# Two fused layers on one core: the passage to the output products, the fill operands and the first pair reordered

## The chip, the core and the metric

One core of a Trainium2 chip runs the whole program in one launch. The metric is the device time in microseconds from start to end of an execution; several executions are timed and their median counts. TensorE is called PE here, VectorE DVE, ScalarE ACT, GpSimd POOL; SP is the engine whose queue issues nearly all DMAs.

## The reference

```python
def phi(x):                                   # q, k, v: 8 x 8 heads x 576 x 64; w_phi: 64 x 128
    proj = einsum('bhsd,df->bhsf', x, w_phi)
    proj = proj - max(abs(proj), axis=-1)
    return concatenate([exp(proj), exp(-proj)], axis=-1)
q_p, k_p = phi(q), phi(k)
kv, z = einsum('bhsf,bhsd->bhfd', k_p, v), k_p.sum(axis=2)
x = (q_p @ kv) / (q_p @ z + 1e-6)             # then 4608 tokens x 512
xn = x / sqrt(mean(x*x) + 1e-6) * rms_g
g, val = xn @ w_gate, xn @ w_val              # 512 -> 1536
out = (g * sigmoid(g) * val) @ w_out          # 1536 -> 512
```

## The kernel before, in words

All products run on PE in a split form of fp32: an operand x becomes a high part (a cast on ACT, line 60) and a low part (x minus the high part, line 61, on DVE or POOL), and a product is three matmuls: high by high, high by low, low by high.

**Attention (lines 190 to 550).** 32 pairs of heads pass through a software pipeline. `front` transposes k, q and the 64 rows left over of both (`rb`) on PE (line 298), splits them and projects them with w_phi (lines 311 to 313, one PSUM tile `pp` of two for each call of `proj`); DVE takes the maximum (315) and subtracts it (318). `mid` takes the exponentials on ACT (338, 378, 379), sums kv on PE (351), and POOL makes the low parts `ql` of q's features (383, 385). `back` multiplies with kv (418), sends the denominators through DRAM (`dd`, `dr`, `di`) and back as `rc`; `last` multiplies by `rc` (455, 456; for the last pair but one on POOL) and stores `xs`. A scheduler orders each engine's instructions in this stage by its own estimate of readiness.

**Fill products.** Into this stage are mixed the products of `xs` with the first three column blocks of w_gate and w_val, for 18 blocks of 256 tokens. `fill` (line 470) splits a block's operands (tile `xo`, two buffers) and returns six units of 12 matmuls each (line 487). `landed` calls it when at most 3 units are left (lines 532 and 533), and once more behind the loop (545). The six units left at the end of the attention stage, and eight more blocks, follow as ordered work.

**Gate and value products (lines 1085 to 1170).** From here a planner (`Flow`) writes every engine's order by hand-given durations; its instructions carry line 563 in the profile. For 9 blocks of 512 tokens and 9 column blocks each, `Unit` makes seven products of a fast 2 by 2 scheme (six matmuls each) in PSUM banks A, B, E; its result `h` (three buffers) is stored into the DRAM tensor `hs`. `scales` makes the token scales with two matmuls on PE ("T" tasks). In the last two blocks the freed weight buffers take the split operands of w_out (`make_o`, the last one built in the tile `x`), and `hload(0)` reads the first 256 tokens of `hs` back as one DMA of 1536 KB into the buffer of weight block 5; `hload(1)` follows in program order.

**Output products (lines 1164 to 1280).** The scheduler orders again. For each of 18 groups `gi` of 256 tokens, `operands` makes seven split operands out of the four blocks a11, a12, a21, a22 of h: casts on ACT, sums on DVE (1191 to 1199, tiles `st`), low parts of a11 and a12 on DVE, the other five on POOL. `omm` runs 18 matmuls for each of the seven products (126 a group) into `fp`, `gy`, `gz`, `gd`. The tiles of this stage lie at the addresses of tiles of the stage before: first 16 buffers `xo` of 3 KB, then the two `st`; those over the last-used `x` wait for it.

## Time and profile before

| | us |
|---|---|
| median of 3 runs | 1263.27 (1262.48 to 1271.12) |
| the profiled execution | 1265.73 |
| its span, first to last instruction | 1264.0 |
| PE busy in the span | 1221.1 (97%) |
| attention with the mixed fill products | about 0 to 494 |
| fill products behind it | about 494 to 560 |
| gate and value products | about 560 to 988 |
| output products | 991.3 to 1259 |

A row of the timeline gives the start, the duration, the engine, the line, the operation with output and inputs, a count where several are merged, and in brackets how long the engine sat idle before it and what released it. Matmuls overlap, so a merged row's duration is longer than the sum of the starts' distances.

### The profile page before, as it was taken

How to read it: one execution, taken by the hardware profiler on the slowest of the kernel's cores; microseconds unless marked ns; L12 is line 12 of the kernel's file. 1: busy time of each engine (PE TensorE's matmuls, PEld its weight loads, DVE VectorE, ACT ScalarE, POOL GpSimd, SP SyncE). 2: the span in 40 equal slices, each digit the busy share in tenths (PEclk: the TensorE clock that was granted, in tenths of full speed). 3: DMA queues.
4: the chain of work that ended last, by engine and by line, in shares of the span. 5: the costliest groups of instructions: out<-in, count | busy, mean ns of one | idle time of the engine just before them, and what ended most of it. 6: DMA issues, size and time to landing. Idle time of an engine off the chain costs nothing.

```text
span 1264.0 us, 28426 instructions
## 1 busy us (share of the span) xinstructions
PE 1221.1 (97%) x10355; PEld 1206.9 (95%) x10355; DVE 1040.8 (82%) x1495; ACT 803.5 (64%) x1865; POOL 836.9 (66%) x758
## 2 busy tenths in 40 slices
PE   7999999999999998999999999999999699999998
PEld 6998999999999998899999999999999699999998
DVE  6888987788878885387986988798876789999994
ACT  5887887778787894666566666667656343434341
POOL 3655665555665666764876875676566578888884
PEclk9999999999999999999999999999999899999999
DMA  5455576565666637675365556655545445444521
GB/s 150 132 127 152 144 200 174 159 176 153 183 167 171 175 102 220 184 239 175 127 200 195 182 194 203 200 176 181 183 146 167 144 147 165 139 134 160 166 93 51
DMA packets 214297, 206.55 MB, mean 163 GB/s; under 512 B 70287, under 2 KB 176655, under 8 KB 214157
## 3 DMA queue, kind: packets, MB, share of 16 engines
q1 hardware_dynamic: 214156, 204.73, 53.7%
q8 instruction: 82, 1.34, 0.4%
q14 instruction: 59, 0.48, 0.1%
HBM read 135.18 MB, written 69.49 MB: 162 GB/s over the span
## 4 chain that ended last, share of the span: by engine, by line
PE 54%; DVE 3%; DMA 1%; issue 1%; POOL 1%; ACT 1%; DVEq 0%; ACTq 0%; POOLq 0%
PE B L563 12%; PE E L563 10%; PE A L563 10%; PE gd L1241 6%; PE gz L1241 6%; PE gy L1241 5%; PE fp L1241 3%; PE fp L487 1%; DMA hs<-h 1%; PE fp L563 1%; DVE wc L563 1%; DMA gvs<-fo 1%; POOL xo L61 0%; PE S L563 0%; DVE xo L61 0%
## 5 line engine op out<-in xcount | busy, mean ns | idle before, releaser
L383 POOL TENSOR_TENSOR ql<-eq,qh 128x256 fp32r<-128x256 f32 x256 | 219.3, 887 | 84.5 <-ACT qh L379 43.4
L563 PE MATMUL B<-xo,w 128*128 128x256 f32 x1458 | 195.0, 278 | 3.9 <-ACT h L563 1.9
L563 PEld LDWEIGHTS B<-xo,w 128*128 128x128 f32 x1458 | 179.4, 188 | 5.3 <-DVE c L563 2.8
L61 POOL TENSOR_TENSOR xo<-st,xo 128x768 fp32r<-128x768 f32 x54 | 126.4, 2355 | 39.9 <-ACT xo L60 38.1
L563 POOL TENSOR_TENSOR h<-h,c 128x256 f32<-128x256 f32 x81 | 65.4, 808 | 114.2 <-ACT h L563 87.2
L60 ACT CAST xo<-st 128x768 fp32r<-128x768 f32 x54 | 43.5, 836 | 150.6 <-DVE st L1194 73.4
L563 PE MATMUL A<-xo,w 128*128 128x256 f32 x972 | 137.7, 277 | 0.3 <-ACT B L563 0.3
L563 PE MATMUL E<-xo,w 128*128 128x256 f32 x972 | 137.7, 277 | 0.0
L315 DVE TENSOR_REDUCE mx<-pp 128x4 f32<-128x512 f32 (+1 forms) x160 | 100.8, 632 | 42.7 <-PE pp L313 41.0
L351 PE MATMUL acc<-vm,ek 128*128 128x65 f32 x1024 | 130.0, 269 | 0.3 <-ACT ek L338 0.2
L351 PEld LDWEIGHTS acc<-vm,ek 128*128 128x128 f32 x1024 | 126.0, 193 | 0.9 <-ACT ek L338 0.9
L563 PEld LDWEIGHTS A<-xo,w 128*128 128x128 f32 x972 | 123.3, 188 | 0.8 <-ACT B L563 0.5
L563 PEld LDWEIGHTS E<-xo,w 128*128 128x128 f32 x972 | 123.1, 188 | 0.2 <-DVE h L563 0.2
L379 ACT ACTIVATE qh<-sm 128x512 fp32r<-128x512 f32 (+1 forms) x192 | 97.3, 507 | 0.0
L61 POOL TENSOR_TENSOR xo<-w,xo 128x768 fp32r<-128x768 f32 x36 | 91.6, 2544 | 0.0
L311 PE MATMUL pp<-wh,th 128*128 128x256 f32 x288 | 87.2, 304 | 4.6 <-DVE yr L318 2.6
L378 ACT ACTIVATE eq<-sm 128x512 f32<-128x512 f32 x128 | 78.5, 614 | 16.5 <-PE sm L367 16.5
L313 PE MATMUL pp<-wh,tl 128*128 128x256 f32 x288 | 83.5, 297 | 0.0
L312 PE MATMUL pp<-wl,th 128*128 128x256 f32 x288 | 81.3, 283 | 0.0
L385 POOL TENSOR_TENSOR ql<-eqr,qh 128x256 fp32r<-128x256 f32 x32 | 24.6, 767 | 81.9 <-ACT qh L379 77.5
L1241 PE MATMUL gy<-w,xo 128*128 128x256 f32 x648 | 77.8, 278 | 0.2 <-ACT xo L60 0.2
L338 ACT ACTIVATE ek<-yk 128x512 f32<-128x512 f32 x128 | 75.4, 650 | 3.9 <-DVE yk L318 3.8
(188 smaller groups left out, 3560.9 us busy)
## 6 DMA issues: line engine op xcount, KB each, us to landing
w<-hs SPq DMA_DIRECT2D x18, 1536.0 KB
hs<-h SPq DMA_DIRECT2D x81, 256.0 KB
gvs<-fo SPq DMA_DIRECT2D x108, 128.0 KB
gvr<-gvs SPq DMA_DIRECT2D x54, 256.0 KB
x<-xs SPq DMA_DIRECT2D x18, 512.0 KB
x<-xs SPq DMA_DIRECT2D x9, 1024.0 KB
rc<-di SPq DMA_DIRECT2D x31, 288.0 KB
kt<-in_k_dram SPq DMA_DIRECT2D x32, 256.0 KB
```

The costliest lines, as they stand in the source:

```text
L61: (lo_eng or nc.vector).tensor_tensor(lo, x, hi.bitcast(F32), ALU.subtract)
L311: nc.tensor.matmul(o, th[:, cs], wh, start=True, stop=False)
L312: nc.tensor.matmul(o, th[:, cs], wl, start=False, stop=False)
L313: nc.tensor.matmul(o, tl[:, cs], wh, start=False, stop=True)
L315: nc.vector.tensor_reduce(mx[:, 0:2 * m], pp[:, 0:2 * m], axis=AX.X, op=ALU.max, apply_absolute_value=True)
L338: nc.scalar.activation(e[h][:, sg], y["k", h], AF.Exp, scale=1.0 - 2.0 * sg)
L351: nc.tensor.matmul(acc[:, sg, h], e[h][:, sg, j], vm[:, h, j], start=False, stop=(h == 1 and j == T0 - 1))
L378: nc.scalar.activation(ei[:, sg], yi, AF.Exp, scale=1.0 - 2.0 * sg)
L379: nc.scalar.activation(hi[:, sg], yi, AF.Exp, scale=1.0 - 2.0 * sg)
L383: nc.gpsimd.tensor_tensor(lo[:, sg, cs], ei[:, sg, cs], hi[:, sg, cs].bitcast(F32), ALU.subtract)
L563: r = f(*a, **k)
L1241: nc.tensor.matmul(place[n], a[:, kp], w[:, o], start=(first and kp == 0 and i == 0), stop=(kp == KP - 1 and i == 2), skip_group_check=True)
```

## The change

It does eight things. (1) The first pair's `front` is in the order k, q, k's projections, then the left-over rows and q. (2) `landed` is called when at most 6 units are left; behind the loop only when fewer than 6 are. (3) A "T" task counts as ready 0.8 us later for the planner. (4) `hload(0)` is four DMAs of 384 KB with points of the unit order as their earliest places; `hload(1)` is a task of the planner. (5) Four of nine `xo` buffers of the gate stage and eight of sixteen of the output stage are skipped at first, and `st` lies ahead of `xo`, so that the buffers used first lie elsewhere. (6) In the first group the low parts of s2 and s3 go to DVE, and its first sum is recorded behind the last instructions of the other engines, so that the low parts of a11 and a12 stand ahead of it. (7) In the first group `omm` takes the high-by-high and high-by-low matmuls of the first five pieces first. (8) The last group's last sum is in two halves.

```diff
-        return [lambda: trans("r" if pr else "k"), lambda: trans("k" if pr else "r"),
+        if pr == 0:
+            return [lambda: trans("k"), lambda: trans("q"), lambda: proj("k", 0), lambda: proj("k", 2),
+                    lambda: trans("r"), lambda: proj("r", 0), lambda: proj("q", 0), lambda: proj("q", 2)]
+        return [lambda: trans("r"), lambda: trans("k"),
...
-        if len(units) <= 3:
+        if len(units) <= 6:
             landed(nc.vector if i < PR else nc.gpsimd)
...
-    if here:
+    if here and len(units) < 2 * J1:
...
-            r = max([0.0] + [d["done"] + self.HOP for d in deps])
+            r = max([0.0] + [d["done"] + self.HOP for d in deps]) + (0.8 if e == "T" else 0.0)
...
+    XSKIP, OSKIP = 4, 8
...
+    for _ in range(XSKIP):
+        xp.tile([128, 2, 2, HT], F32R, name="xo")
...
-    def hload(gi):
-        j = LAST[HSLOT[gi % 3]]
-        h = side_of(j).tile([128, NJ, 256], F32, name=f"w{j}")
-        tc.nc.sync.dma_start(out=h, in_=hsv[:, :, gi * 256:(gi + 1) * 256])
-        hts[gi] = h
+    def hload(gi, m=0, of=1):
+        if m == 0:
+            j = LAST[HSLOT[gi % 3]]
+            hts[gi] = side_of(j).tile([128, NJ, 256], F32, name=f"w{j}")
+        js = slice(m * NJ // of, (m + 1) * NJ // of)
+        tc.nc.sync.dma_start(out=hts[gi][:, js], in_=hsv[:, js, gi * 256:(gi + 1) * 256])
...
-            flow.add("Q", 7.0, lambda: hload(0), after=tuple((NB - 1, LAST[HSLOT[0]], n) for n in ROW))
+            j0, j1 = (LAST[HSLOT[gi]] for gi in range(2))
+            for m, last in enumerate(((j0, 4), (j0 + 2, 5), (j0 + 1, 3), (j0 + 2, 6))):
+                flow.add("Q", 2.0, lambda m=m: hload(0, m, 4), after=tuple((NB - 1, j0, n) for n in ROW) + ((NB - 1, *last),))
+            flow.add("Q", 7.0, lambda: hload(1), after=tuple((NB - 1, j1, n) for n in ROW))
...
-    hload(1)
...
+    ost = ctx.enter_context(tc.tile_pool(name="ost", bufs=2, reuse_waits="tile"))
     xop = ctx.enter_context(tc.tile_pool(name="oop", bufs=16, reuse_waits="tile"))
-    ost = ctx.enter_context(tc.tile_pool(name="ost", bufs=2, reuse_waits="tile"))
+    for _ in range(OSKIP):
+        xop.tile([128, KP, 128], F32R, name="xo")
...
-            nc.vector.tensor_tensor(t["s3"], a11, a21, ALU.subtract)
+            with nullcontext() if lo2 is nc.gpsimd else late():
+                nc.vector.tensor_tensor(t["s3"], a11, a21, ALU.subtract)
...
-            split("s2", t["s2"], nc.gpsimd)
+            split("s2", t["s2"], lo2)
...
-            split("s3", t["s3"], nc.gpsimd)
+            split("s3", t["s3"], lo2)
...
-                        [128, KP, 128], ost)
+                        [128, KP, 128], ost, nc.gpsimd if gi else nc.vector)
...
-            for kp in range(KP):
+            turns = [(kp, i) for kp in range(KP) for i in range(3)]
+            if gi == 0:
+                turns.sort(key=lambda t: (t[0] == KP - 1, t[1] == 2))
+            for kp, i in turns:
...
-        nc.vector.tensor_tensor(ro[:, 1:3], D, uu, ALU.add)
+        if todo:
+            nc.vector.tensor_tensor(ro[:, 1:3], D, uu, ALU.add)
+        else:
+            for b in range(2):
+                nc.vector.tensor_tensor(ro[:, 1 + b], D[:, b], uu[:, b], ALU.add)
```

What it moves, at three places. On POOL, the end of the attention stage before: `ql` are the low parts of the last pairs, `xo<-x,xo` those of a fill block (two instructions a block), `nd<-nd,rc` the division of the last pair but one.

```order
L383 TENSOR_TENSOR ql<-eq,qh 128x256 x4
L61 TENSOR_TENSOR xo<-x,xo 128x512 x2
L383 TENSOR_TENSOR ql<-eq,qh 128x256 x4
L385 TENSOR_TENSOR ql<-eqr,qh 128x4x64
L383 TENSOR_TENSOR ql<-eq,qh 128x256 x4
L61 TENSOR_TENSOR xo<-x,xo 128x512 x2
L455 TENSOR_TENSOR nd<-nd,rc 64x576
L456 TENSOR_TENSOR nd<-nd,rc 64x576
L61 TENSOR_TENSOR xo<-x,xo 128x512 x2
```

The same place now:

```order
L386 TENSOR_TENSOR ql<-eq,qh 128x256 x8
L388 TENSOR_TENSOR ql<-eqr,qh 128x4x64
L386 TENSOR_TENSOR ql<-eq,qh 128x256 x4
L61 TENSOR_TENSOR xo<-x,xo 128x512 x4
L458 TENSOR_TENSOR nd<-nd,rc 64x576
L459 TENSOR_TENSOR nd<-nd,rc 64x576
```

One fill block's low parts left this stretch for an earlier place, and both others stand ahead of the division. On PE, of the 144 fill matmuls that stood behind the last projection (line 313), 81 still do; the 63 others stand earlier. On SP, the loads of h before (`w<-hs`, the first is `hload(0)`), with the stores `hs<-h` of the units' results between them:

```order
L1021 DMA w_14764<-hs 128x12x256
L893 DMA hs<-h 128x512 x2
L1021 DMA w_14924<-hs 128x12x256
L893 DMA hs<-h 128x512
L1021 DMA w_15156<-hs 128x12x256
```

And now:

```order
L1029 DMA w_14768<-hs 128x3x256 x2
L899 DMA hs<-h 128x512
L1029 DMA w_14768<-hs 128x3x256 x2
L899 DMA hs<-h 128x512
L1029 DMA w_14901<-hs 128x12x256
L899 DMA hs<-h 128x512
L1029 DMA w_15171<-hs 128x12x256
```

Ahead of the first store stand two quarters of the load instead of the whole. On DVE, the start of the output stage before (`w` there is h as loaded, `xo<-w,xo` the low parts of a11 and a12):

```order
L563 TENSOR_TENSOR w_14828<-wc,w_14828 128x1024
L1191 TENSOR_TENSOR st<-w_14764 128x768
L61 TENSOR_TENSOR xo<-w_14764,xo 128x768
L1192 TENSOR_TENSOR w_14764<-w_14764 128x6x128
L61 TENSOR_TENSOR xo<-w_14764,xo 128x768
L1194 TENSOR_TENSOR st<-w_14764 128x768
L1199 TENSOR_TENSOR st<-w_14764,st 128x768
```

And now:

```order
L566 TENSOR_TENSOR w_14835<-wc,w_14835 128x1024
L61 TENSOR_TENSOR xo<-w_14768,xo 128x768 x2
L1204 TENSOR_TENSOR st<-w_14768 128x768
L1205 TENSOR_TENSOR w_14768<-w_14768 128x6x128
L1207 TENSOR_TENSOR st<-w_14768 128x768
L61 TENSOR_TENSOR xo<-st,xo 128x768 x2
L1212 TENSOR_TENSOR st<-w_14768,st 128x768
```

The two low parts stand ahead of the sums, and two low parts more (of s2 and s3) behind them.

## Rows read from the trace of the kernel before

**Rows 1.** The page: busy time by engine, and PE's granted clock in 40 slices.

```profile
PE 1221.1 (97%) x10355; PEld 1206.9 (95%) x10355; DVE 1040.8 (82%) x1495; ACT 803.5 (64%) x1865; POOL 836.9 (66%) x758
...
PEclk9999999999999999999999999999999899999999
```

**Rows 2.** Stretches of 20 us: length, busy us (instructions) by engine, granted clock, DMA share, GB/s.

```profile
0.00:20.00 20.00, 11.72 (x70) 11.11 (x71) 11.13 (x26) 6.89 (x14) 3.96 (x18) 1.00 0.53 137
...
260.00:280.00 20.00, 19.16 (x165) 18.96 (x164) 17.09 (x30) 16.71 (x44) 9.84 (x13) 1.00 0.61 180
...
500.00:520.00 20.00, 17.19 (x130) 16.60 (x129) 0.00 (x0) 7.87 (x18) 11.51 (x8) 0.90 0.65 195
...
980.00:1000.00 20.00, 12.77 (x84) 11.76 (x83) 12.68 (x20) 8.06 (x15) 8.05 (x6) 0.83 0.65 216
...
1200.00:1220.00 20.00, 20.00 (x179) 20.00 (x179) 19.90 (x13) 9.13 (x13) 18.18 (x9) 1.00 0.41 135
```

**Rows 3.** Timeline of the first pair, PE.

```profile
7.24 0.45 PE L298 MATMUL sm<-ident,rb 128*128 128x128 f32 x1 [2.50 <-DMA rb<-in_q_dram]
...
8.19 0.56 PE L311 MATMUL pp<-wh,th 128*128 128x256 f32 x1
...
12.59 0.55 PE L311 MATMUL pp<-wh,th 128*128 128x256 f32 x1 [2.13 <-DVE yr L318]
```

**Rows 4.** Timeline behind the attention stage, PE, in two answers.

```profile
494.53 0.39 PE L487 MATMUL fp<-xo,fg 128*128 128x256 f32 x1 [0.98 <-ACT xo L60]
...
495.88 0.96 PE L487 MATMUL fp<-xo,fg 128*128 128x256 f32 x6 [0.85 <-POOL xo L61]
...
506.92 0.38 PE L563 MATMUL fp<-xo,fg 128*128 128x256 f32 x1 [1.02 <-ACT xo L60]
...
508.80 0.95 PE L563 MATMUL fp<-xo,fg 128*128 128x256 f32 x6 [1.50 <-POOL xo L61]
...
517.79 1.52 PE L563 MATMUL fp<-xo,fv 128*128 128x256 f32 x12
...
519.15 1.52 PE L563 MATMUL A<-xo,fg 128*128 128x256 f32 x12
```

**Rows 5.** Timeline of the same stretch, POOL.

```profile
486.41 3.34 POOL L383 TENSOR_TENSOR ql<-eq,qh 128x256 fp32r<-128x256 f32 x4
...
504.50 1.42 POOL L455 TENSOR_TENSOR nd<-nd,rc 64x576 f32<-64x576 f32 x1 [6.83 <-DMA xs<-nd]
```

**Rows 6.** The chain that ended last: the store of h; the last products and last sum.

```profile
975.23 9.73 DMA hs<-h
...
1254.95 4.09 PE gd L1241 x36
1259.06 0.69 DVE ro L1270
```

**Rows 7.** Timeline of the passage to the output products, all engines.

```profile
985.04 0.38 ACT L563 ACTIVATE h<-A 128x256 f32<-128x256 f32 x1 [3.43 <-DMA hs<-h]
...
985.74 0.97 PE L563 MATMUL B<-xo,w 128*128 128x256 f32 x6 [1.93 <-ACT h L563]
...
989.47 1.04 ACT L563 CAST w<-x 128x1024 fp32r<-128x1024 f32 x1 [1.12 <-DVE x L563]
...
990.59 2.37 POOL L563 TENSOR_TENSOR w<-x,w 128x1024 fp32r<-128x1024 f32 x1 [1.44 <-ACT w L563]
...
991.30 0.51 PE L1241 MATMUL fp<-w,xo 128*128 128x256 f32 x2 [3.04 <-ACT xo L60]
...
992.99 0.96 DVE L1191 TENSOR_TENSOR st<-w 128x768 f32<-128x768 f32 x1 [2.42 <-POOL w L563]
...
993.87 0.95 DVE L61 TENSOR_TENSOR xo<-w,xo 128x768 fp32r<-128x768 f32 x1
...
1000.32 2.59 DVE L1199 TENSOR_TENSOR st<-w,st 128x768 f32<-128x768 f32 x1 [2.89 <-POOL xo L61]
...
1010.50 1.21 PE L1241 MATMUL fp<-w,xo 128*128 128x256 f32 x8 [2.26 <-DVE xo L61]
```

More of the change, by code (lines that the diff above doesn't have):

```diff
@@ L1 @@
-from contextlib import ExitStack, contextmanager
+from contextlib import ExitStack, contextmanager, nullcontext
 import concourse.bass as bass
@@ L671 @@
     sub = lambda eng, o, a, b, op=ALU.subtract: eng.tensor_tensor(o, a, b, op)
-    ring = {"wc": [None, None], "gvr": (3, []), "xo": (9, []), "S": (1, []), "ld": None, "r": None}
+    for _ in range(XSKIP):
+        xp.tile([128, 2, 2, HT], F32R, name="xo")
+    ring = {"wc": [None, None], "gvr": (3, []), "xo": (9, [()] * XSKIP), "S": (1, []), "ld": None, "r": None}
     def seven(raw, tile, s4, s3, s2, s1, own=True, prompt=False):
@@ L1071 @@
     flow.free.update(V=8.0, P=4.0)
+    tc.LEFT = len(units), len(blocks_left), len(here)
     flow.pri = -2
@@ L1094 @@
         n += 1
-        if len(units) % (2 * J1) == 0:
-            flow.marks.add(("fill", len(units) // (2 * J1) and -2 or -1))
+        if len(units) in (0, 2 * J1):
+            flow.marks.add(("fill", -2 if units else -1))
         flow.step(1.9)
@@ L1168, with operands @@
     ps_f = ctx.enter_context(tc.tile_pool(name="ps_o", bufs=2, space=PSUM))
+    ost = ctx.enter_context(tc.tile_pool(name="ost", bufs=2, reuse_waits="tile"))
     xop = ctx.enter_context(tc.tile_pool(name="oop", bufs=16, reuse_waits="tile"))
-    ost = ctx.enter_context(tc.tile_pool(name="ost", bufs=2, reuse_waits="tile"))
+    for _ in range(OSKIP):
+        xop.tile([128, KP, 128], F32R, name="xo")
     ow = ctx.enter_context(tc.tile_pool(name="ow", bufs=2, reuse_waits="tile", side="right"))
     ps_g = ctx.enter_context(tc.tile_pool(name="ps_g", bufs=2, reuse_waits="tile", space=PSUM))
-    def operands(a11, a12, a21, a22, part, pool):
+    def operands(a11, a12, a21, a22, part, pool, lo2):
         ops = {}
@@ L1237, in omm @@
             (xh, xl), o = ops[OPS[n][0]], OPS[n][1]
-            for kp in range(KP):
+            turns = [(kp, i) for kp in range(KP) for i in range(3)]
+            if gi == 0:
+                turns.sort(key=lambda t: (t[0] == KP - 1, t[1] == 2))
+            for kp, i in turns:
                 wh, wl = wos_ops[kp]
-                for i, (a, w) in enumerate(((xh, wh), (xh, wl), (xl, wh))):
-                    nc.tensor.matmul(place[n], a[:, kp], w[:, o], start=(first and kp == 0 and i == 0),
-                                     stop=(kp == KP - 1 and i == 2), skip_group_check=True)
+                a, w = ((xh, wh), (xh, wl), (xl, wh))[i]
+                nc.tensor.matmul(place[n], a[:, kp], w[:, o], start=(first and (kp, i) == turns[0]),
+                                 stop=((kp, i) == turns[-1]), skip_group_check=True)
         if gi in (1, 2, 4, 9):
```

## The prediction

> **What bounds the kernel now.** I read the page first. PE is busy for 97% of the span and every other engine for at most 82% [rows 1], so only what leaves PE idle, or lowers its clock, costs time, and the question at each edit is which of PE's waits it ends. The stretches of 20 us show where PE idles: the reader is to compare the first figure behind the length with 20. A stretch of the steady output stage has 20.00 at clock 1.00; the first 20 us have 11.72, those at 500 us 17.19 at clock 0.90, those at 980 us 12.77 at clock 0.83 [rows 2]. These three places are the ones that the change touches. Over the whole span PE idles 1264.0 - 1221.1 = 42.9 us [rows 1]; the three stretches hold 8.3 + 2.8 + 7.2 = 18.3 of it, and their clock costs (1 - 0.90) x 20 = 2.0 and (1 - 0.83) x 20 = 3.4 us more, since half of PE's 2.4 GHz is granted for a while there. Then I read the timeline of each place for what ended each wait.
>
> A scale first. Two units of fill products start 519.15 - 517.79 = 1.36 us apart [rows 4]; they have 12 matmuls, so a matmul of 256 columns takes 0.113 us at full clock. An output group of 126 matmuls takes 14.28 us, and 18 groups 257.0.
>
> **The first pair.** PE does k's transposes and then waits 2.50 us for the left-over rows [rows 3], because theirs stand next; the first projection starts at 8.19. In the new order q's transposes and two projection matmuls stand ahead of that wait. Both fit into it if q has landed; the next ones go on at about 7.5 instead of 8.19, and two matmuls of about 0.2 us (here at half clock) are done: 0.7 + 0.4 = 1.1 us. k's first maximum is then also earlier, and so is the release of the PSUM tile for which PE waits 2.13 us at 12.59 [rows 3]. Bounds: if none of the first wait is filled, nothing is gained there and q's maximum comes later than now, +1; if both waits close, -4.6. I take -1.5, near the working.
>
> **The fill operands.** The 12 units between 494.53 and 519.15 take 24.6 us, with the wait of 0.98 ahead of them 25.6 [rows 4], where 12 x 1.36 = 16.3 would do: 9.3 us are lost. 4.35 us of that are the four waits of these rows, on casts by ACT and low parts by POOL, which are recorded so late that they stand behind the last numerators and the division; the rest is mostly half clock behind the waits [rows 2]. In the new order the first block's casts stand ahead of the last exponentials, and both blocks' low parts ahead of the division, for which POOL idles until 504.50 [rows 5]. All four waits lose their cause. What is late next? 63 matmuls, 63 x 0.113 = 7.1 us, no longer stand beside the last pair's numerators, where POOL's low parts set the pace (the last four end at 486.41 + 3.34 = 489.75 [rows 5]). They run earlier instead, where PE is nearly full, so the tail begins about 7 us later. POOL has one block's two low parts less in the tail (each 1.25 to 1.5 us), so its last `ql` ends at about 487 on the old scale, 494 on the new one; the first block's low parts follow at once, PE waits for them 1 to 2 us, and both blocks are done at about 495.5 + 16.3 = 511.8. The next block's low parts stand on POOL behind the division, which needs `rc`; its load stands in SP's queue behind the copies of the first block's fourth unit (at about 501.5), some 4 us later than now, so POOL divides at about 507 to 509 and PE waits another 0 to 1. Forecast: of 9.3 us 3.3 stay, -6.0. Bounds: -9.3, all of it; and, if the tail idles for all of the 7.1 us that covered it, with one more spell of half clock (2.0) and the division 2 later, -9.3 + 7.1 + 2.0 + 2.0 = +1.8. I take the value nearer to the first end because the waits' causes are gone by the order, while POOL's own work in the tail got less.
>
> **The scale matmuls** counted ready 0.8 us later by the planner stand a little later on PE. Nothing shows more than about one short wait by them in a stretch; I set 0, with 1 us to either side for another order of the whole stage.
>
> **The store of h.** `hload(0)`, 1536 KB, is issued just ahead of a unit's store, which then takes 9.73 us [rows 6]; the next user of that buffer is a SiLU on ACT that sits 3.43 us, and PE waits 1.93 for it [rows 7]. Two quarters ahead of the store instead of four leave about half: 9.73 / 2 = 4.9 us, from about 976 to 981, and the SiLU could start at 985.04 - 3.43 = 981.6. The wait goes: -1.9. Bounds: -2.4 with the short gap behind it, 0 if the later quarters hold the store up as much.
>
> **The passage.** Of PE's wait of 3.04 us before 991.30 [rows 7] nothing goes: the chain is the last gate products, the last sum of w_out's operands on DVE, its cast on ACT (989.47, 1.04 us) and only then the cast of a11, and that order on ACT is as before. Behind 991.30 the ideal is 257.0 us and four pairs of wide matmuls of 0.46, 258.9 in all; the last products end at 1254.95 + 4.09 = 1259.04 [rows 6], 267.7 later, so 8.8 us are lost: half clock for some 7 us (3.4), the wait for the low part of a11, and 2.26 us at 1010.50, where the second group's products stand ahead of 34 matmuls of the first that were ready [rows 7]. DVE sat 2.42 us until POOL's last low part had left the tile under `st`, and only then did a11's low part begin, 993.87 [rows 7].
>
> In the new order DVE begins the two low parts right behind a11's cast, at about 991.3, 2.6 us earlier, and PE has 20 matmuls of high parts to do first. At half clock these take about 4.5 us, so the low parts are in time; 16 more bring PE to 997.6, and by then DVE has done the three sums behind them (four operations of 0.95 [rows 7] from 993), so s2's cast is ready as well. From there I follow PE's rows with 0.113 us a matmul and the later operands with 0.95 us a DVE operation while POOL is idle and 2.59 while it works [rows 7]: the first group ends at about 1008.3, the second waits 0.7 us for a11's low part and 1.7 for a12's, which DVE does behind a sum and an output sum. 1008.3 + 17 x 14.28 + 3 x 0.46 + 2.4 = 1254.9: -4.1 against 1259.04. Bounds: -8.8; and if every one of the first group's four new or moved DVE operations takes 2.59 instead of 0.95, 4 x 1.64 = 6.6 come back, +2.5.
>
> The rule that weighs against this is the Trainium skill's: by the GPSIMD Engine Reference, Specifications, GpSimd shares its SBUF interfaces with VectorE and contends with DVE instructions that read two SBUF tensors. The same operation of 768 columns has 0.95 us beside an idle POOL and 2.59 beside a working one [rows 7], so the trace agrees. By the rule, low parts moved from POOL to DVE only help while POOL has nothing to do.
>
> **The last sum** in two halves leaves half of 0.69 us [rows 6] behind the last matmul: -0.3, between 0 and -0.5.
>
> **The sum.** -1.5 - 6.0 - 1.9 - 4.1 - 0.3 = -13.8. The profiled execution has a span of 1264.0 and 1.73 around it; the new span is 1250.2, its time 1251.9. It was 2.46 us above the median of the runs, 1263.27, so the forecast for a median is 1249.5, 1.1% less. 1% is 12.6 us, about what a measurement of this kernel can tell from no change.
>
> **The rivals.** *The tail starves.* What the fill operands gain is lost again in the attention tail without its 63 matmuls, and the term is 0: 1249.5 + 6.0 = 1255.5. For it: POOL sets the tail's pace. Against: PE's cover is moved, not added to, and POOL's tail is shorter.
>
> *The passage is bound by DVE and POOL together.* The moved low parts meet POOL's own and the 4.1 us do not come: 1253.6. For it: 2.59 us against 0.95. Against: POOL has three low parts instead of five in the first group.
>
> *The attention stage is ordered worse: slower.* Everything behind the first pair is ordered anew, all 23 stretches of 20 us to 480 us. If each had one more wait of the size of that at 260 us, 20 - 19.16 = 0.84 [rows 2], this would cost 23 x 0.84 = 19.3: 1268.8, slower than before. It decides from 13.8 / 23 = 0.6 us a stretch. Against: the same scheduler orders the same work, and few stretches have such a wait now.
>
> *All waits close.* First pair -4.6, fill -9.3, store and passage -1.9 - 8.8, last sum -0.3: -24.9, 1238.4. Against: the wait of 3.04 us and some half clock stay.
>
> **Chances.** Forecast 0.45, starving tail 0.25, bound passage 0.15, all waits (or nearly) 0.09, worse order 0.06. Faster by over 1% is below 1250.6: nearly all of the last-but-one, most of the forecast (its own range is 1246 to 1253) and a little of the two partial ones, 0.09 + 0.36 + 0.07 = 0.52; slower by over 1% comes from the worse order in its heavier half and mishaps of its kind, 0.05; within 1% is the rest, 0.43. The range takes the forecast and both partial cases with some 3 us of another order to either side: 1242.5 to 1259.
>
> **What would show it.** Right: in the new profile the first 20 us have over 13 us of PE; between 490 and 520 us waits on ACT and POOL for `xo` sum to under 2.5 us and the clock stays near 1; the store behind the first load takes about 5 us and PE has no wait on that SiLU; about 3 us of wait and a clock below 1 stay at the passage; the second group waits under 3 us. Wrong: waits on `ql` above 4 us in the last pair, or waits on DVE in the second output group above 5, or PE's busy share between 20 and 480 us clearly lower than before.

## The result and the profile after

The median of six runs is 1250.91 us (1248.15 to 1257.59) against 1267.99 us of the kernel before in six runs (1262.48 to 1271.12). The ratio is 0.9882 with a 95% interval from 0.9846 to 0.9918: faster by 1.2%. The forecast was 1249.5 us with a range of 1242.5 to 1259, and faster by over 1% was its likeliest case; the measured median lies in the range. The profiled execution has 1250.33 us and a span of 1248.6, 15.4 us less than 1264.0.

The page after, the lines that answer to [rows 1]: busy time by engine, and PE's granted clock in 40 slices.

```profile
PE 1216.2 (97%) x10355; PEld 1204.6 (96%) x10355; DVE 1034.0 (83%) x1498; ACT 803.3 (64%) x1867; POOL 830.8 (67%) x756
...
PEclk9999999989999998999999999999999899999999
```

PE is as full as before, and two slices of low clock stand in the first half where there were none. The stretches after, columns as in [rows 2]:

```profile
0.00:20.00 20.00, 14.63 (x83) 13.21 (x84) 12.15 (x28) 8.18 (x17) 4.16 (x19) 1.00 0.51 137
...
240.00:260.00 20.00, 16.97 (x121) 16.27 (x120) 11.57 (x21) 10.84 (x29) 8.79 (x11) 0.83 0.69 178
260.00:480.00 220.00, 219.49 (x1870) 218.56 (x1869) 180.26 (x318) 177.30 (x446) 130.30 (x159) 1.00 0.57 160
480.00:520.00 40.00, 35.23 (x277) 34.33 (x276) 21.89 (x20) 22.28 (x55) 27.55 (x27) 0.91 0.65 211
...
980.00:1000.00 20.00, 18.87 (x136) 18.49 (x137) 16.68 (x15) 7.53 (x11) 8.52 (x4) 0.83 0.42 139
```

Three of these stretches of the kernel before, as they were not all shown:

```profile
240.00:260.00 20.00, 19.04 (x159) 18.62 (x158) 13.87 (x25) 13.08 (x34) 8.98 (x11) 1.00 0.51 143
260.00:480.00 220.00, 216.76 (x1832) 214.13 (x1831) 185.92 (x325) 179.65 (x450) 134.95 (x166) 1.00 0.58 159
480.00:520.00 40.00, 35.26 (x259) 33.55 (x260) 12.85 (x9) 16.82 (x41) 24.37 (x21) 0.91 0.73 225
```

The reader is to see three things. The first 20 us gained 2.9 us of PE. The stretch from 260 to 480 us gained 2.7, which no step of the prediction had. And from 480 to 520, where the largest term was to come, PE's busy time and clock are what they were.

Two markers cut the span: the first matmul into PSUM bank A behind the fill products (519.15 before [rows 4], 515.15 after) and the first output matmul (991.30 [rows 7], 980.62). So 4.0 of the 15.4 us came up to the first, 6.7 between the two and 4.7 behind the second. The experiments were read by the same markers, each in one profile; e9, the same program as after, has the first marker at 514.10, so a difference of about 1 us there is within what one program shows.

### The profile page after: what moved, and what is told of

The parts are those of the page before. It is cut to its first block, busy times and chain, and to the rows that moved or that the text cites. A ratio compares the mean times of both kernels' runs of the same rounds, so it can differ in the third digit from the quotient of the medians.

```text
span 1248.6 us, 28447 instructions
## 1 busy us (share of the span) xinstructions
PE 1216.2 (97%) x10355; PEld 1204.6 (96%) x10355; DVE 1034.0 (83%) x1498; ACT 803.3 (64%) x1867; POOL 830.8 (67%) x756
## 4 chain that ended last, share of the span: by engine, by line
PE 83%; DVE 7%; DMA 4%; issue 2%; ACT 1%; POOL 1%; SPq 1%; DVEq 0%; ACTq 0%; POOLq 0%
PE B L566 12%; PE E L566 11%; PE A L566 11%; PE acc L354 6%; PE fp L490 5%; PE gd L1257 5%; PE gz L1257 5%; PE gy L1257 5%; PE sm L421 5%; PE fp L1257 3%; PE pp L311 2%; PE pp L313 2%; PE pp L312 2%; PE sm L370 2%; PE sm L298 2%
## 5 line engine op out<-in xcount | busy, mean ns | idle before, releaser
L386 POOL TENSOR_TENSOR ql<-eq,qh 128x256 fp32r<-128x256 f32 x256 | 216.4, 875 | 92.9 <-issue 57.6
L61 POOL TENSOR_TENSOR xo<-st,xo 128x768 fp32r<-128x768 f32 x52 | 122.4, 2366 | 35.4 <-ACT xo L60 31.7
L566 ACT ACTIVATE h<-A 128x256 f32<-128x256 f32 x81 | 31.1, 384 | 76.8 <-PE A L566 63.3
```

What stands on the lines that cost most here:

```text
L61: (lo_eng or nc.vector).tensor_tensor(lo, x, hi.bitcast(F32), ALU.subtract)
L386: nc.gpsimd.tensor_tensor(lo[:, sg, cs], ei[:, sg, cs], hi[:, sg, cs].bitcast(F32), ALU.subtract)
L566: r = f(*a, **k)
```

## The experiments

All start from the changed kernel; e1, e2, e5, e6, e7 and e12 undo one part of the change, e3, e4, e8, e10 and e11 mend something, and e9 is the changed kernel itself. All ratios are to the kernel before on the same chip.

**e1: the first pair's old order.**

```diff
-            return [lambda: trans("k"), lambda: trans("q"), lambda: proj("k", 0), lambda: proj("k", 2),
-                    lambda: trans("r"), lambda: proj("r", 0), lambda: proj("q", 0), lambda: proj("q", 2)]
+            return [lambda: trans("k"), lambda: trans("r"), lambda: proj("r", 0), lambda: proj("k", 0),
+                    lambda: trans("q"), lambda: proj("k", 2), lambda: proj("q", 0), lambda: proj("q", 2)]
```

> The changed kernel with the first pair in the old order (left-over rows right behind k's transposes); all else as changed. The starts of the pairs 8 to 16 lie on average 2.7 us earlier in the changed kernel than in the kernel before. Theory: that lead is the first pair's, so here these pairs start 2 to 3 us later than in the changed kernel, PE's first 20 us are back near 11.7 us (from 14.6), and the span is 1.5 to 3 us longer than 1248.6. Rival: the pairs behind the first are bound by DVE and ACT and make the lead good without the reorder, then the pairs 8 to 16 start within 0.7 us of the changed kernel's and the span is the same. Second question: the hole at 249 to 253 us (waits of 1.71 and 1.31 and a granted clock of 0.83, which the kernel before does not have) is still there if it belongs to the earlier fill units, and gone if it belongs to the new order of the first pair.

Span 1250.9, ratio 0.9917 (0.9893 to 0.9942). The first 20 us fall back to the 11.7 of before:

```profile
0.00:20.00 20.00, 11.52 (x66) 10.91 (x67) 10.70 (x26) 6.89 (x14) 3.96 (x18) 1.00 0.54 137
```

Pairs 1 to 6 (counted from 0, by their first exponentials on ACT) begin 2.8 us later than in the changed kernel, and bank A 2.1 later (517.25). Pairs 8 to 16, which the theory named, begin 5.1 us later: the granted clock from 90 to 120 us is 0.89 here and 1.00 after, so that a spell of half clock lies between. The hole of the second question is there with the old order too (17.58 us of PE from 240 to 260), at clock 1.00. The new order is worth 2 to 3 us, to about 1 us, since pairs 1 to 6 begin 1.0 us later in e9 than in after.

**e2: the old placing of the fill operands.**

```diff
-        if len(units) <= 6:
+        if len(units) <= 3:
...
-    if here and len(units) < 2 * J1:
+    if here:
```

> The changed kernel with the fill operands split as before (at 3 units left, and once more behind the loop); all else as changed. Theory: the wait of 4.44 us at 495 us (PE for the last pair's numerators) shrinks below 1 us because fill products again stand beside it, and the waits on casts and low parts of the fill operands, 4.35 us in the kernel before, are back; the first product in bank A starts 3 to 5 us later than in the changed kernel (515.15) if the hole at 250 us stays, 0 to 2 later if the hole goes with the edit. Prediction as put on record: 6 us longer than the changed kernel. Rival (the starving tail gives back all): the same span as the changed kernel within 1 us.

Span 1253.8, ratio 0.9934 (0.9901 to 0.9967); bank A at 517.93, 2.8 later than after. Pairs 1 to 6, ahead of anything that the edit touches, already begin 0.6 us later. Its stretches, and PE's timeline behind the attention stage:

```profile
240.00:260.00 20.00, 16.73 (x130) 16.52 (x130) 13.27 (x24) 11.30 (x30) 8.82 (x11) 0.91 0.53 152
260.00:480.00 220.00, 217.24 (x1839) 214.76 (x1837) 186.73 (x326) 179.96 (x451) 134.71 (x165) 1.00 0.57 158
```

```profile
495.00 0.39 PE L490 MATMUL fp<-xo,fg 128*128 128x256 f32 x1 [0.98 <-ACT xo L60]
...
496.35 0.96 PE L490 MATMUL fp<-xo,fg 128*128 128x256 f32 x6 [0.84 <-POOL xo L61]
...
506.29 0.38 PE L566 MATMUL fp<-xo,fg 128*128 128x256 f32 x1 [1.02 <-ACT xo L60]
...
508.31 2.71 PE L566 MATMUL fp<-xo,fg 128*128 128x256 f32 x11 [1.64 <-POOL xo L61]
```

The four waits of [rows 4] are back (0.98 + 0.84 + 1.02 + 1.64 = 4.5 us), so the edit does end them. The wait of 4.44 us at the last numerators, to which e3 comes, is not there: PE has no wait above 0.1 us from 481 to 495. The hole at 240 to 260 us is still there. The stretch from 260 to 480 us is back near the value of before: 217.24 with the old placing, 219.49 to 219.51 in all twelve profiles with the new placing. The matmuls that the edit moved fill 2.3 us of short gaps there.

**e3 and e4: the last pair's numerators in tiles of their own; then also a fill block's low parts on DVE.** In the changed kernel one wait had taken the place of the four. DVE's, ACT's and PE's rows after, from the timeline of the last pair:

```profile
491.95 0.79 DVE L458 TENSOR_TENSOR nd<-nd,rc 64x576 f32<-64x576 f32 x1 [4.86 <-DMA rc<-di]
...
492.77 1.71 DVE L459 TENSOR_TENSOR nd<-nd,rc 64x576 f32<-64x576 f32 x1
...
494.56 0.89 ACT L424 ACTIVATE nd<-sm,epsd 128x320 f32<-128x320 f32 x2 [4.32 <-issue]
...
495.14 0.58 PE L421 MATMUL sm<-qh,kv1h 128*128 128x256 f32 x1 [4.44 <-ACT nd L424]
```

PE waits 4.44 us for ACT's copy of the numerators. That copy starts at 494.56, behind DVE's division of an earlier pair, which ends at 492.77 + 1.71 = 494.48 and reads tiles of the same ring of four `nd`; DVE itself waited 4.86 for the reciprocals' way through DRAM. "Issue" in ACT's row (idle time for which the profile shows no releaser) hides that release.

```diff
-        nd = [big.tile([128, S], F32, name="nd", bufs=4) for _ in range(2)]
+        nd = [big.tile([128, S], F32, name="nd", bufs=4) if pr < PR - 1 else wk.tile([128, 2, T0, F], F32, name="ek").rearrange("p a t f -> p (a t f)")[:, 0:S] for _ in range(2)]
```

> The changed kernel with the last pair's numerators in the two buffers of the exponentials (tile ek, free by then) instead of tile nd, whose buffers are still held until the last pair but two is divided. Theory: ACT's copy of the numerators sat 4.32 us behind that division (it ends at 494.48, the copy starts at 494.56), and PE's wait of 4.44 us is that; here it goes, PE waits at most 2 us for the low parts that POOL ends at 493.9 and 495.6, the first product in bank A starts at about 511.4 instead of 515.15 and the span is about 3.7 us shorter. Rival 1: ACT waited for something else (order behind the exponentials), then the 4.4 us stay. Rival 2: the fill operands' low parts and the next load take the wait's place, then the start in bank A moves by less than 1.5 us.

Span 1251.5, ratio 0.9921 (0.9889 to 0.9952). Timeline, ACT, PE and POOL:

```profile
490.53 0.93 ACT L424 ACTIVATE ek<-sm,epsd 128x320 f32<-128x320 f32 x2
...
511.62 1.39 POOL L458 TENSOR_TENSOR nd<-nd,rc 64x576 f32<-64x576 f32 x1 [4.78 <-DMA gvs<-fo]
...
514.90 1.32 POOL L566 TENSOR_TENSOR xo<-x,xo 128x512 fp32r<-128x512 f32 x1
...
516.28 1.44 PE L566 MATMUL A<-xo,fg 128*128 128x256 f32 x5 [4.43 <-POOL xo L566]
```

The numerators now start at 490.53 without a wait, 4.0 earlier, which shows the cause. But PE meets a wait of 4.43 some 25 us on: a low part stands on POOL behind the last division. The wait moved, and nothing was gained: 510.89, where bank A starts, and 4.43 make 515.3, against 515.15 after. e4 adds the cure for that one:

```diff
-            landed(nc.vector if i < PR else nc.gpsimd)
+            landed(nc.vector if i <= PR + 1 else nc.gpsimd)
```

> As the run before, and the low parts of the fill block in the tail on DVE instead of POOL, ahead of the division for which DVE idles 4.86 us (487.1 to 491.95). Theory: with the low parts done by about 491 the fill products stand between the last numerators and nothing of the 4.44 us and its half clock is left: first product in bank A 5 to 6 us earlier than 515.15, span 5 to 6 us shorter than the changed kernel's. Rival: the next block's load and split become the bound behind, then no more than the 3.7 us of the run before.

Bank A starts at 505.88 with one wait of 1.48 behind it, so effectively at 507.4, 7.8 us earlier than after; the first output matmul at 972.70, 7.9 earlier. Its window:

```profile
480.00:520.00 40.00, 36.59 (x306) 35.64 (x306) 27.67 (x32) 24.36 (x60) 26.70 (x22) 1.00 0.72 234
```

Yet the span is 1249.4, no less than after's 1248.6, and the ratio 0.9897 (0.985 to 0.9944). The gain went behind 972.70: from there to the end it takes 276.7 us against 268.0. Why stands in the last section: PE ran its matmuls there at a slower cadence, at the same granted clock.

**e5: the whole load of h again.**

```diff
-            for m, last in enumerate(((j0, 4), (j0 + 2, 5), (j0 + 1, 3), (j0 + 2, 6))):
-                flow.add("Q", 2.0, lambda m=m: hload(0, m, 4), after=tuple((NB - 1, j0, n) for n in ROW) + ((NB - 1, *last),))
+            flow.add("Q", 7.0, lambda: hload(0), after=tuple((NB - 1, j0, n) for n in ROW))
```

> The changed kernel with the first load of h again as one DMA of 1536 KB; all else as changed. Theory: the store of h behind it again takes about 9 us, the SiLU that takes its buffer sits 3 to 4 us, PE's wait of 1.9 us ahead of the third last product is back, and from the SiLU three products earlier to the first output matmul it takes 12.4 to 12.8 us (12.6 in the kernel before, 10.8 in the changed one): 1.9 us more. Rival: the planner's later place for the load hides it anyway, then 10.8 as now.

Span 1253.6, ratio 0.988 (0.9798 to 0.9962). The SiLU on ACT, which waits for the store behind that load:

```profile
978.03 0.39 ACT L566 ACTIVATE h<-A 128x256 f32<-128x256 f32 x1 [1.10 <-DMA hs<-h]
```

It waits 1.10 us instead of 3.43 [rows 7], and PE not at all. From the store's issue (970.56) to that start it is 7.5 us, where the store of before took 9.73 [rows 6]. ACT's wait belongs to the whole load: both profiles that have it show one, 3.43 and 1.10, and none of the twelve with the load in quarters has one above 0.3 us. But here it costs PE nothing: whether PE waited hung on how fast that one transfer landed, so that PE's 1.93 us aren't shown to be the edit's in full.

**e6, e7, e8: the parts of the passage.** e6 undoes the edits of the order with the new buffers (on DVE this isn't quite the order of before: the two low parts now stand behind all three sums), e7 has the new order with the old buffers. e8 puts the first four operand tiles where the units' `x`, their last-used tile, does not lie. Each has two runs (ratios 0.9853, 0.9881 and 0.9872, each to about 0.01), too few to tell them from after by time, so they are read by profile.

```diff
# e6
-                        [128, KP, 128], ost, nc.gpsimd if gi else nc.vector)
+                        [128, KP, 128], ost, nc.gpsimd)
...
-            if gi == 0:
-                turns.sort(key=lambda t: (t[0] == KP - 1, t[1] == 2))
# e7
-    XSKIP, OSKIP = 4, 8
+    XSKIP, OSKIP = 0, 0
...
-    ost = ctx.enter_context(tc.tile_pool(name="ost", bufs=2, reuse_waits="tile"))
     xop = ctx.enter_context(tc.tile_pool(name="oop", bufs=16, reuse_waits="tile"))
+    ost = ctx.enter_context(tc.tile_pool(name="ost", bufs=2, reuse_waits="tile"))
# e8
-    XSKIP, OSKIP = 4, 8
+    XSKIP, OSKIP = 4, 0
...
-    ost = ctx.enter_context(tc.tile_pool(name="ost", bufs=2, reuse_waits="tile"))
-    xop = ctx.enter_context(tc.tile_pool(name="oop", bufs=16, reuse_waits="tile"))
+    xop = ctx.enter_context(tc.tile_pool(name="oop", bufs=15, reuse_waits="tile"))
+    xo1 = ctx.enter_context(tc.tile_pool(name="oo1", bufs=1, reuse_waits="tile"))
+    ost = ctx.enter_context(tc.tile_pool(name="ost", bufs=2, reuse_waits="tile"))
...
-            h, l = (xop.tile(part, F32R, name="xo") for _ in range(2))
+            h, l = xop.tile(part, F32R, name="xo"), (xo1 if n == "a22" else xop).tile(part, F32R, name="xo")
```

> The changed kernel with the operands of the first output group in the old order (first sum ahead of the low parts, low parts of s2 and s3 on POOL, three products of each piece of w_out together); buffers as changed. Theory: from the first output matmul to the end of the span it takes about 4.5 us more than in the changed kernel (268.0 there, 272.7 before), with a wait of about 2 us on DVE's first low part and one of about 2 us in the second group. Rival (DVE and POOL together bind the passage in any order): within 1 us of 268.0.

> The changed kernel without the skipped buffers (0 and 0 instead of 4 and 8) and with the tile st behind xo again; all else as changed. The addresses in the two programs show that the skips change none, and that with st ahead of xo three of the first four operand tiles (low part of a11, both parts of a12) lie over x, with st behind only the low part of a11. Theory: this edit cost a little instead of gaining: here ACT casts a12 at once behind a11 (1.74 us of waiting gone), PE's 0.52 us ahead of the second product goes, and the passage from the first output matmul on is the same or up to 1 us shorter; the units up to there run as before the edit. Rival (the edit does what it says): DVE starts its first low part later than 1.7 us behind the first matmul and the passage is 1 us or more longer.

> The changed kernel with the operand tiles of the first four pieces really off x: 15 shared buffers and one of a22's low part alone at the top, st behind it (it is written later). Theory: ACT casts a12 at once, DVE's first low part starts within 0.3 us of a11's cast (now 1.68 us behind the first matmul, with a wait of 2.42 us on POOL), PE's 0.52 us goes, but the span gets only 0.5 to 1 us shorter, since PE has 20 products of high parts to do at half clock meanwhile. Rival 1: DVE's low parts beside POOL's last one take 2.6 us instead of 0.92 and PE waits for them, then up to 2 us longer. Rival 2: the single buffer of a22's low part holds up the later groups, then longer by 18 times a wait.

The rows of the changed kernel to compare with, the passage on POOL, ACT, DVE and PE:

```profile
979.91 2.36 POOL L566 TENSOR_TENSOR w<-x,w 128x1024 fp32r<-128x1024 f32 x1 [1.44 <-ACT w L566]
...
982.30 0.83 ACT L60 CAST xo<-w 128x768 fp32r<-128x768 f32 x1 [1.74 <-POOL w L566]
...
982.30 1.83 DVE L61 TENSOR_TENSOR xo<-w,xo 128x768 fp32r<-128x768 f32 x2 [2.42 <-POOL w L566]
...
987.02 0.83 ACT L60 CAST xo<-st 128x768 fp32r<-128x768 f32 x1 [3.89 <-DVE st L1207]
...
980.62 2.06 PE L1257 MATMUL fp<-w,xo 128*128 128x256 f32 x10 [3.04 <-ACT xo L60]
...
983.19 2.50 PE L1257 MATMUL gy<-w,xo 128*128 128x256 f32 x10 [0.52 <-ACT xo L60]
...
1011.97 2.11 PE L1257 MATMUL gd<-w,xo 128*128 128x256 f32 x16 [0.18 <-POOL xo L61]
```

From the first output matmul to the end of the span it is 268.0 us after, 270.0 in e6, 267.9 in e7 and 267.8 in e8. So the order alone (e7) gives all of the passage's gain. Of the 4.7 us to before's 272.7, 0.9 are the slow cadence of the last section and 0.4 the last sum in halves (the span ends 4.5 us behind PE's last matmul, before 4.9); undoing the order brings back 2.0, and what the rest hangs on was not separated. e6 shows the waits that the order covers:

```profile
985.69 0.80 PE L1257 MATMUL gy<-w,xo 128*128 128x256 f32 x2 [2.75 <-ACT xo L60]
987.50 3.68 PE L1257 MATMUL fp<-w,xo 128*128 128x256 f32 x16 [1.02 <-DVE xo L61]
```

The buffers gain no time beside the new order. One reason stands in the rows after: DVE still waits 2.42 us for POOL's last low part (as in [rows 7]), and ACT's cast of a12 1.74, because the tiles moved off one place and onto it again: in the program's addresses the units' `x` lies at 150496 to 158688, before under a11's low part and both `st`, after under a11's low part and both of a12's. So point (5) of the change did not put the tiles used first elsewhere. e8 moves these away, and its rows are POOL's, DVE's and ACT's:

```profile
980.92 2.37 POOL L566 TENSOR_TENSOR w<-x,w 128x1024 fp32r<-128x1024 f32 x1 [1.44 <-ACT w L566]
...
981.60 3.37 DVE L61 TENSOR_TENSOR xo<-w,xo 128x768 fp32r<-128x768 f32 x2 [0.71 <-ACT xo L60]
...
987.94 0.83 ACT L60 CAST xo<-st 128x768 fp32r<-128x768 f32 x1 [5.63 <-DVE st L1208]
```

The wait is gone, but the two low parts now run beside POOL and take 3.37 us where they took 1.83: no gain. The Trainium skill's rule (GPSIMD Engine Reference, Specifications: GpSimd contends with VectorE instructions that read two SBUF tensors) stands beside this; these rows agree with it. The same two engines set the pace in e7, whose rows are ACT's and PE's:

```profile
992.76 0.83 ACT L60 CAST xo<-st 128x768 fp32r<-128x768 f32 x1 [5.82 <-DVE st L1207]
...
993.64 1.42 PE L1257 MATMUL gy<-w,xo 128*128 128x256 f32 x10 [1.39 <-ACT xo L60]
```

The first cast of a sum stands behind DVE's low parts and sums. It comes 987.02 - 980.62 = 6.4 us behind the first output matmul after, 6.5 in e7 (first matmul at 986.26) and 6.3 in e8 (at 981.62), wherever the tiles lie. In e7 and e8 PE is there early and waits 1.39 and 1.23 us for it; in after it comes just in time, as its clock was half for longer (0.83 from 980 to 1000, in e7 and e8 0.91) and it waited 0.52 for a12.

**e9 and e10: the changed kernel again, and with its first weights held back.** Rows after at 245 us, DVE and PE:

```profile
245.10 0.76 DVE L566 TENSOR_TENSOR wc<-wc 128x256 f32<-128x256 f32 x2 [5.33 <-DMA wc<-wvs]
...
249.66 0.35 PE L311 MATMUL pp<-wh,th 128*128 128x256 f32 x1 [1.71 <-DVE yq L318]
...
253.18 1.12 PE L370 MATMUL sm<-ident,yq 128*128 128x128 f32 x4 [1.31 <-DVE tl L61]
```

A difference of weights for the gate stage, 270 us ahead of its use, stands so early in DVE's queue that DVE waits 5.33 us for its load; PE starves behind it. e10 lets the first of them go no earlier than DVE's last attention instruction:

```diff
-            self.sync = tc.nc.sync
+            self.sync, self.vector.last = tc.nc.sync, next(i for i in reversed(tc.nc.cur_bb.bb.instructions) if i.engine == E.DVE)
```

> The changed kernel once more, unaltered, to see what differs between two executions of one program. Theory: everything up to the hole at 245 to 260 us lies within 0.5 us of the first profile, the hole itself costs between 0.7 us (no half clock) and 4.5 us (half clock), the wait of 4.4 us at the last numerators is there again, and stretches in which a matmul of 256 columns takes 117.8 ns instead of 113.3 at a granted clock of 1.00 may stand elsewhere or not at all (the kernel before had one from 718 to about 800 us, 3 us of its span). Rival: the hole and the pace belong to the program, then both are the same in both profiles.

> The changed kernel with DVE's first operation of the gate and value stage (differences of the first weight block, two of 0.38 us) held behind the attention stage's last on DVE. Theory: in every run so far DVE sits 3.1 to 6.1 us at 240 to 247 us for the load of these weights, and what PE waits behind it (1.8 to 4.1 us, and half clock in several runs) goes with it: PE's waits between 235 and 270 us sum to under 1 us, its clock there is 1.00, and the pair that starts its exponentials at 258.0 in the changed kernel starts at 253 to 254.5. Span 1 to 4.5 us shorter than 1248.6. Rival: the waits are the attention stage's own (maxima and subtractions on DVE), then they stay at 1.8 us or more.

e9 (the same program) has 17.00 us of PE from 240 to 260 at clock 1.00, where after had 16.97 at 0.83: the wait belongs to the program, the half clock behind it does not stand in every execution. Two things more differ between these profiles of one program. Pairs 1 to 6 begin 1.0 us later in e9, where the theory allowed 0.5; and the slow cadence of the last section costs 4.8 us in e9 and 0.9 after. The hole belongs neither to the first pair's order nor to the fill's placing, as e1 and e2 have it too. In e10 the stretch is full:

```profile
240.00:260.00 20.00, 20.00 (x175) 20.00 (x174) 15.78 (x27) 15.23 (x41) 9.58 (x12) 1.00 0.77 213
```

Span 1241.9, median 1246.04 us (1243.7 to 1247.16), ratio 0.9828 (0.9806 to 0.9850), e9 beside it 1252.21 and 0.9872 (0.9849 to 0.9895). One line beats both kernels: its four runs are all shorter than e9's six (1248.16 to 1254.90), and bank A starts at 510.23 against e9's 514.10. Of these 3.9 us 3.0 are PE's in this stretch; of the other 4.9 us between the two profiles 4.2 are the cadence.

**e11: e4 and e10 together, and a low part on DVE that e4 had waited for.**

```diff
-        l1 = flow.add("PV", dict(P=1.5, V=0.9), lambda eng: lo(eng, 2), h1)
+        l1 = flow.add("PV", dict(P=1.5, V=0.9), lambda eng: lo(eng if m else nc.vector, 2), h1)
```

> The changed kernel with four mends: own buffers for the last numerators, the tail's fill low parts on DVE, the first weight differences behind the attention stage, and the second low part of the next fill block on DVE too (it stood behind POOL's division, 1.48 us of PE's wait). Theory: the first product in bank A at 503 to 506 us without a wait behind it (515.15 in the changed kernel), first output matmul at 968 to 971, and 268 from there: span 1236 to 1240 at full pace, 8 to 12 us below the changed kernel's, ratio to the kernel before about 0.980. Rival: what is won ahead of the units is lost in them (their loads and scales are not ready), then the first output matmul comes at 974 or later.

Span 1241.1, median 1247.13 (1242.86 to 1255.33), ratio 0.9845 (0.9817 to 0.9874): the two can't be told apart. Bank A starts 4.6 us earlier than in e10 (505.61), the first output matmul only 0.7 (973.29, behind the theory's 968 to 971). Of the 3.9 us that the units took longer, 3.4 are the slow cadence of the last section; and a wait is left in the fill, of ACT for a store and of PE for ACT:

```profile
499.27 0.37 ACT L566 COPY fo<-fp 128x256 f32<-128x256 f32 x1 [3.25 <-DMA gvs<-fo]
499.70 1.64 PE L566 MATMUL fp<-xo,fg 128*128 128x256 f32 x12 [1.41 <-ACT fo L566]
```

**e12: the scale matmuls counted ready as before.**

```diff
-            r = max([0.0] + [d["done"] + self.HOP for d in deps]) + (0.8 if e == "T" else 0.0)
+            r = max([0.0] + [d["done"] + self.HOP for d in deps])
```

> The changed kernel without the 0.8 us by which the planner counts the scale matmuls ready later. Theory: the two waits of these matmuls on DVE (0.89 and 0.47 us in the kernel before, none in the changed one) come back in this size, the first output matmul comes 0 to 2 us later relative to the first product in bank A (465.5 us in the changed kernel, 472.2 before with 3 us of slow pace in it). Rival: they don't come back, and the term is 0.

Span 1260.1, ratio 0.9917 (0.9883 to 0.9951). PE's waits for DVE ahead of the scale matmuls are back, 0.89 here and 0.48 at 887.63, as before (0.89 and 0.47):

```profile
716.15 0.73 PE L566 MATMUL S<-t,ones 128*128 128x512 f32 x2 [0.89 <-DVE xo L566]
```

The number is worth these 1.4 us. The slow cadence costs 9.0 us in e12's profile, and two of its stretches begin behind these two waits (717 to 803 and 888 to 987 us). In the profile before, too, a stretch begins behind the first of them and lasts to 804:

```profile
717.07 0.73 PE L563 MATMUL S<-t,ones 128*128 128x512 f32 x2 [0.89 <-DVE xo L563]
```

No profile without the wait has a stretch that begins there. So the number may be worth some 3 us more by the cadence; two profiles don't show it, since e9 has 4.8 us of the cadence without these waits.

## Why the prediction came out right

The total was right, 13.8 us forecast and 15.4 between the two profiles, but with one large term too big and gains that it didn't have. That the median came within 1.4 us of the forecast is partly luck: the kernel before measured 1267.99 here and 1263.27 when the forecast was worked out, so the medians lie 17.1 apart.

- **First pair, forecast -1.5: -2.3.** Pairs 1 to 6 begin on average 2.3 us earlier than before. In the timeline after, the first projection starts at 5.63 instead of 8.19, and the waits of [rows 3] shrank to 1.05 and 0.53:

```profile
5.63 0.80 PE L311 MATMUL pp<-wh,th 128*128 128x256 f32 x2
...
7.47 0.45 PE L298 MATMUL sm<-ident,rb 128*128 128x128 f32 x1 [1.05 <-DMA rb<-in_q_dram]
...
10.59 0.55 PE L311 MATMUL pp<-wh,th 128*128 128x256 f32 x1 [0.53 <-DVE yk L318]
```

  The mechanism held: both waits shrank, by 1.45 and 1.60 us, where 1.1 in all was worked out. The prediction calls the matmuls here half clock; they do start 0.21 us apart (8.15, 8.36 and 8.57 us after), but the granted clock on record for the first 20 us is 1.00 [rows 2], and why they are slow is not shown.
- **Fill operands, forecast -6.0: -2.8 (e2).** The step that failed is "what is late next". POOL's `ql` was named, and the last numerators came: they wait for `nd` tiles held by an earlier pair's division (shown by e3). Before, the 63 matmuls stood beside that division and covered it. So in the tail the rival of the starving tail was nearly right. Of the 9.3 us 6.7 stayed: the wait of 4.44, and 2.3 of half clock behind it, since the 20.0 us from 495.14 to 515.15 hold 17.7 us of matmuls at full clock. e2, with the old placing, loses 517.93 - 495.00 + 0.98 - 16.3 = 7.6 us there (its clock from 480 to 520 is 0.96, that of before 0.91), so the edit took only 0.9 from the tail. What saved the term is that the 63 matmuls did not just push the tail back by 7 us, as worked out: they filled gaps from 260 to 480 us (2.3 us by e2, 2.7 against before). Of the signs named, that for the waits on `xo` came; that for the clock did not (0.89 from 490 to 520 us, as before).
- **The hole at 245 us, not forecast: +1.1 as a remainder.** Bank A came 4.0 us earlier, which leaves 4.0 - 2.3 - 2.8 = -1.1 for it and what else is between. By its own rows it cost more: PE's busy time fell from 19.04 to 16.97 and the clock from 1.00 to 0.83; in return a spell of half clock at 98 us is gone (0.94 from 90 to 120 us before, 1.00 after). The hole was in the kernel before, where DVE waits 3.55 us for the same load, and no step of the prediction had it. The rival of a worse order had this kind of loss, in one stretch instead of 23.
- **Scale matmuls, forecast 0: -1.4 (e12).** Two of their waits went, beyond the bound of 1 us; what they do to the cadence is open.
- **Store of h, forecast -1.9: between 0 and -1.9.** PE's wait is gone after, but gone in e5 as well; only ACT's is shown to follow the whole load.
- **Passage, forecast -4.1: -3.4, and last sum, forecast -0.3: -0.4,** without the cadence. The wait of 3.04 stayed as forecast. The waits of 0.7 and 1.7 us in the second group did not come (its largest row above is 0.18), but half clock lasted longer (0.83 over 980 to 1000 us, which is half clock for 6.8 us, where the working had 4.5); and DVE's low parts begin 982.30 - 980.62 = 1.7 us behind the first output matmul instead of with it, since the new place is not free. The step's reason was wrong there and its size right. The rival of DVE and POOL together named what sets the pace, by the cast 6.3 to 6.5 us behind the first matmul in after, e7 and e8, but its price of 4.1 us did not come.
- **The cadence, not forecast: -3.6,** not shown to follow from any edit: e9, the same program as after, has 4.8 us of it, before 4.5. Without it the profiles differ by 11.8 us, 0.9%. The medians differ by more, 17.1; how much of that is cadence and hole in the runs without a profile stays open.

With the store's 1.9 us these terms sum to -14.7; 0.7 of the 15.4 us are not placed.

So right for partly wrong reasons: the fill's shortfall of 3.2 us was made up by the scale matmuls and the cadence, the latter by luck as far as is shown.

## What to carry to other kernels

When an edit moves work out of a stretch, ask what that work covered there, and follow each tile ring of the stretch to its last reader; a wait named "issue" can be such a release. Look on every engine's queue for an instruction of a later stage that waits for its load: holding one back was worth 3 to 4 us here (PE's busy time from 240 to 260 us and bank A, e10 against e9), about as much as the largest part of the change. Buffers should be checked by their addresses, and two profiles of one program should be compared before a difference of 3 us is explained.

## What the hardware showed that was not expected

At a granted clock of 1.00, which is 2.4 GHz, PE ran the same matmuls at one of two cadences. The chains of e10 and e4, groups of 36 matmuls of 256 columns in the output stage:

```profile
1229.21 4.08 PE gz L1257 x36
```

```profile
1236.42 4.24 PE gz L1257 x36
```

That is 4.08 / 36 = 113.3 ns a matmul against 4.24 / 36 = 117.8 ns. PE has no waits in either, and e4 stays at 4.24 through nearly its whole output stage, which costs about 9.7 us. Where the cadence changed in the rows read, a wait of PE or the wide matmuls of the scales and sums mostly stood there; in e5, PE's timeline:

```profile
607.49 0.84 PE L566 MATMUL B<-xo,w 128*128 128x256 f32 x6
...
609.47 0.97 PE L566 MATMUL B<-xo,w 128*128 128x256 f32 x6 [1.14 <-DVE c L566]
...
610.28 0.87 PE L566 MATMUL A<-xo,w 128*128 128x256 f32 x6
...
795.15 0.97 PE L566 MATMUL B<-xo,w 128*128 128x256 f32 x6 [0.41 <-DVE c L566]
...
795.96 0.84 PE L566 MATMUL A<-xo,w 128*128 128x256 f32 x6
```

A wait at 609.47 turns six matmuls from 0.84 to 0.87 us, and one at 795.15 turns them back. But in e9 and e11 the slow cadence also ends within 18 matmuls that show no wait (at 976.6 and 967.7 us). Summed from the first product in bank A to the end, over the matmuls of 256 columns that start 116 to 121 ns behind the one before at granted clock 1.00, the excess over 113.3 ns is 4.5 us in the profile before, 0.9 after, 10.9 in e4, 8.0 in e5, 4.8 in e9, 0.6 in e10 and 9.0 in e12, so it hid e4's gain and e12's true size. What sets the one or the other was not found out. The Trainium skill (TensorE: Matmul & The Clock Gate, Part 1) gives for the warm clock a start-to-start time of N / 2.4 GHz and about 2.5 ns; for 256 columns this makes an estimate of 109.2 ns. The rows here show 113.3 and 117.8, and the measurement decides.
